# PSUM banks of one Q chunk and of the M groups assigned by hand in a fused linear-attention and MLP block

## The chip, the cores and the metric

The kernel runs on one core of one Trainium2 chip. The metric is the device time of one launch in microseconds (us).

Names used throughout: PE is TensorE (matmuls), PEld its weight loads, DVE is VectorE, ACT is ScalarE. PSUM is the memory that matmuls write; this kernel uses it as 8 banks, each of which holds a 128 x 512 fp32 result. In the lines of the chain below, "issue" is time in which an engine waited for nothing that the profile shows.

## The reference

The input is normalised, then goes through linear attention (32 heads of 20) and an MLP; both results are added to the input. Only the attention branch matters here.

```python
phi = lambda t: jnp.where(t > 0, t + 1, jnp.exp(t)) + 1e-6
pq, pk = phi(q), phi(k)
kv  = jnp.einsum("bhsd,bhse->bhde", pk, v)
z   = jnp.einsum("bhsd->bhd", pk)
num = jnp.einsum("bhqd,bhde->bhqe", pq, kv)
den = jnp.einsum("bhqd,bhd->bhq", pq, z)[..., None] + 1e-6
o   = num / den                                   # then o @ wo
# out = x + attention(xn) + mlp(xn), S = 2048, D = 640, F = 1536
```

The kernel never forms `o`: it multiplies the masked `kv` by `wo` first ("M", 640 x 640), so that `num @ wo` becomes `pq @ M` and can share an accumulation with the second MLP product.

## The kernel before

A planner records each operation with what it reads and writes, and puts a semaphore wait wherever an engine needs another's result or reuses its space. A PSUM bank is one of the tracked areas: a matmul that writes a bank waits until everything that read the bank's earlier content is done. `take(n)` hands banks out in a ring.

```python
ring = [0]
def take(n):
    b = ring[0]
    if n == 2 and b % 2:
        b += 1
    b %= 8
    ring[0] = (b + n) % 8
    return b
```

The part between the KV statistics and the output products:

```python
def phi(src, b, nb, dst, res_dst, extra_w):       # cut: index arithmetic
    Pl.ins("scalar", ... activation(e2, src, ACT.Exp), reads=br, ...)            # L463, reads the bank
    Pl.ins(v, ... tensor_scalar(et, et, 1.0, 1e-6, ALU.min, ALU.add), ...)       # L464
    Pl.ins(v, ... scalar_tensor_tensor(out=d2, in0=src, scalar=0.0, in1=e2,
           op0=ALU.max, op1=ALU.add), reads=br + [r_ek[s]], ...)                 # L466, frees the bank

def q_chunk(c):                                    # one chunk = 512 tokens, DT = 5 units
    for j in range(DT):
        b = take(1)
        Pl.ins("tensor", [5 matmuls of 128x512 into bank b], ...)                # L509
        phi(bank(b), b, 1, PQ[:, j, cc], r_PQ[c][j], [])

def z_step():                                      # cut
    ...                                            # L517, then five products ZB on DVE, L523
def kvt_step():                                    # five blocks, one bank each
    ...                                            # L529 on PE, masked copies on DVE, L533

def m_step():
    for j in range(DT):
        b = take(2)                                # a pair of banks for each of 5 groups
        ...                                        # 16 matmuls into 32-partition strips, L545
        Pl.ins("scalar", ... activation(halves(Msb[:, j, :]), pair(b), ACT.Copy),
               reads=B_[b:b + 2], writes=[r_M[j], r_zsum, r_zhl])                # L550, frees the pair

q_chunk(0); z_step(); kvt_step(); q_chunk(1)
q_chunk(2)
m_step()
q_chunk(3)
...
bs = [out_w2(0)]; db = den_step()                  # output products of the MLP; den in 32-partition strips
bs += [out_w2(1), out_w2(2, 0, JT // 2)]           # then the first products with Msb
```

Of the kernel before, what the change touches and what calls it, by code (L numbers as in the profile page):

```python
# [112 lines left out]
def bass_parallel_sum__linear_attn_block__dense_activation_gelu__prompt_kernel(  # L113
# [23 lines left out]
    with contextlib.ExitStack() as es:  # L137
# [44 lines left out]
# [10 lines that stand above are left out]
        def bank(b, lo=0, hi=512):  # L192
            return ps[:, b * 512 + lo: b * 512 + hi]

        def pair(b):
            return ps[:, b * 512:(b + 2) * 512].rearrange("p (a n) -> p a n", a=2)[:, :, 0:HW]

        def halves(ap):
            return ap.rearrange("p (a n) -> p a n", a=2)
# [255 lines left out]
        def phi(src, b, nb, dst, res_dst, extra_w):  # L455
            s = ring_e[0] % 3
            ring_e[0] += 1
            w = D if nb == 2 else CW
            et = ek[:, s, 0:w]
            e2 = halves(et) if nb == 2 else et  # L460
            d2 = halves(dst) if nb == 2 else dst
            br = B_[b:b + nb]
            Pl.ins("scalar", lambda e: e.activation(e2, src, ACT.Exp), reads=br, writes=[r_ek[s]])  # L463
            Pl.ins(v, lambda e: e.tensor_scalar(et, et, 1.0, 1e-6, ALU.min, ALU.add),  # L464
                   reads=[r_ek[s]], writes=[r_ek[s]])
            Pl.ins(v, lambda e: e.scalar_tensor_tensor(out=d2, in0=src, scalar=0.0, in1=e2,  # L466
                                                       op0=ALU.max, op1=ALU.add),
                   reads=br + [r_ek[s]], writes=[res_dst] + extra_w)

        ring_e = [0]  # L470
        for t in range(NT):
            b = take(2)
# [11 lines left out]
        for f in range(DT):  # L484
            b = take(2)
# [19 lines left out]
        def q_chunk(c):  # L505
            cc = slice(c * CW, (c + 1) * CW)
            for j in range(DT):
                b = take(1)
                Pl.ins("tensor", [(lambda e, k=k, j=j, b=b: e.matmul(  # L509
                    bank(b), Wqkv[:, k, j:D:DT], xnT[:, k, cc],  # L510
                    start=(k == 0), stop=(k == DT - 1))) for k in range(DT)],
                    reads=[r_Wq] + r_xnT[c * CH:(c + 1) * CH], writes=[B_[b]])
                phi(bank(b), b, 1, PQ[:, j, cc], r_PQ[c][j], [])
# [12 lines left out]
        def kvt_step():  # L526
            for t in range(DT):
                b = take(1)
                Pl.ins("tensor", [(lambda e, k=k, b=b, t=t: e.matmul(  # L529
                    bank(b, 0, Wd[t]), Wqkv[:, k, 2 * D + t * P:2 * D + (t + 1) * P],  # L530
                    GTb[:, k, e0[t]:e1[t]], start=(k == 0), stop=(k == DT - 1))) for k in range(DT)],
                    reads=[r_Wv] + r_GT, writes=[B_[b]])
                Pl.ins(v, lambda e, b=b, t=t: e.tensor_tensor(  # L533
                    out=KVT[:, t, e0[t]:e1[t]], in0=bank(b, 0, Wd[t]), in1=maskKV[t][:], op=ALU.mult),
                    reads=[B_[b], r_masks], writes=[r_KVT])

        def m_step():
            for j in range(DT):
                b = take(2)
                fns = []  # L540
                for h in range(2):
                    for i in range(2):
                        for q in range(4):
                            c0 = j + 32 * DT * q
                            fns.append(lambda e, t=q + i, q=q, i=i, h=h, b=b, c0=c0: e.matmul(  # L545
                                bank(b + h, 0, HW)[32 * q:32 * q + 32, :],
                                KVT[:, t, c0:c0 + 31 * DT + 1:DT], Wo[:, t, h * HW:(h + 1) * HW],
                                start=(i == 0), stop=(i == 1)))
                Pl.ins("tensor", fns, reads=[r_KVT, r_Wo], writes=B_[b:b + 2])
                Pl.ins("scalar", lambda e, b=b, j=j: e.activation(halves(Msb[:, j, :]), pair(b), ACT.Copy),  # L550
                       reads=B_[b:b + 2], writes=[r_M[j], r_zsum, r_zhl])
# [47 lines left out]
        z_step()  # L599
        kvt_step()  # L600
        q_chunk(1)
        q_chunk(2)
        m_step()
        q_chunk(3)
        for c in range(NC):
            x_again(c)
# [16 lines left out]
        def out_w2(t, lo=0, hi=JT, b=None):  # L623
            b = take(2) if b is None else b
            for i in range(lo, hi):
                Pl.ins("tensor", [mm(b, t, i, 0), mm(b, t, i, 1)], reads=mm_reads(t, i), writes=B_[b:b + 2],
                       mark=(i == JT - 1))
            return b
# [41 lines left out]
        for t in range(3, NT - 1):  # L670
            b = out_w2(t)
# [45 lines left out]
```

## Time and profile before

| | before |
|---|---|
| time, median (range), 6 runs | 210.94 us (210.4 to 211.22) |
| span of the profiled run | 209.0 us |
| PE busy | 204.9 us, 98% |
| chain of waits, by engine | PE 92%, DVE 6% |

From the page of the kernel before: the span, the engines' busy time, and the chain that ended last.

```profile
span 209.0 us, 3950 instructions
...
PE 204.9 (98%) x1599; PEld 141.0 (67%) x1599; DVE 108.8 (52%) x227; ACT 75.1 (36%) x142; POOL 20.2 (10%) x61
...
PE 92%; DVE 6%; issue 1%; DVEq 0%
```

PE is the limit. What can still be saved without removing matmuls is PE's waiting, and the chain says where to look: between the first and the last few microseconds of the kernel it leaves PE for one stretch only. These are some lines of the chain of waits in order of time (start, duration, what):

```profile
111.11 0.24 DVE ZB L523
...
114.28 0.21 DVE ek L464
...
123.54 0.70 DVE PQ L466
124.24 0.14 issue
124.38 1.29 PE ps L545 x32
125.67 5.53 PE ps L509 x25
```

From the ZB products to the fourth group of M, DVE's work is back to back and PE is released by it. DVE is late because the five ZB products and five masked copies stand in its queue ahead of the phi of Q chunk 1. Now the timeline of the same stretch (start, duration, engine, line, what, how many; in brackets the engine's idle time before it and what ended it):

```profile
109.08 0.52 PE L517 MATMUL ps<-onesb,Msb 128*128 128x1 bf16 x10
111.03 10.96 PE L509 MATMUL ps<-xnT,Wqkv 128*128 128x512 bf16 x50
116.57 0.69 DVE L466 SCALAR_TENSOR_TENSOR PQ<-ps,ek 128x512 bf16<-128x512 f32 x1
121.91 1.29 PE L545 MATMUL ps<-Wo,W 128*32 128x320 bf16 x32
122.55 0.69 DVE L466 SCALAR_TENSOR_TENSOR PQ<-ps,ek 128x512 bf16<-128x512 f32 x1
123.38 0.75 PE L545 MATMUL ps<-Wo,W 128*32 128x320 bf16 x16 [0.18 <-DVE PQ L466]
123.54 0.69 DVE L466 SCALAR_TENSOR_TENSOR PQ<-ps,ek 128x512 bf16<-128x512 f32 x1
124.38 1.29 PE L545 MATMUL ps<-Wo,W 128*32 128x320 bf16 x32 [0.24 <-DVE PQ L466]
125.60 5.12 PEld L509 LDWEIGHTS ps<-xnT,Wqkv 128*128 128x128 bf16 x25 [0.25 <-issue]
142.32 4.24 PE L617 MATMUL ps<-Msb,PQ 128*128 128x320 bf16 x30
```

How to read it: Q chunks 1 and 2 run on PE without a break (111.03 on). M's groups 0 and 1 start at 121.91. Group 2 starts at 123.38, just after the phi of Q2 unit 3 ends (122.55 + 0.69 = 123.24), and group 3 at 124.38, just after that of Q2 unit 4 (124.23). From M's start to the first weights of Q chunk 3 it is 125.60 - 121.91 = 3.69 us. The line at 109.08 (the z step) and the first product with Msb at 142.32 are two marks: 33.24 us pass from one to the other.

### The profile page before, as it was taken

The page shows a single profiled execution, that of the slowest core. Times are in us where ns is not written, and L with a number is a line of the kernel's source. Part 1 is how long each engine was busy: PE and PEld are TensorE (multiplying, and loading weights), DVE is VectorE, ACT ScalarE, POOL GpSimd, SP SyncE. Part 2 cuts the span into 40 slices and gives each one's busy share as a digit, 9 for nine tenths or more (in the row PEclk, how much of TensorE's full clock was granted, in tenths as well). Part 3 has the DMA queues.
Part 4 walks back from the last instruction along what each step waited for, and adds up shares of the span by engine and source line. Part 5 has one row for each costly group of instructions (what it writes and reads, how often), then busy time and mean ns, then how long its engine had stood idle before and what let it go on. Part 6 is the DMA issues. An engine that isn't in the chain of part 4 may idle for free.

```text
span 209.0 us, 3950 instructions
## 1 busy us (share of the span) xinstructions
PE 204.9 (98%) x1599; PEld 141.0 (67%) x1599; DVE 108.8 (52%) x227; ACT 75.1 (36%) x142; POOL 20.2 (10%) x61
## 2 busy tenths in 40 slices
PE   7999999999999999999999999999999999999995
PEld 2799987444457777777756565577777777777775
DVE  4589970000008888999178975478633522523322
ACT  2689887666676444111253576100000000000000
POOL 3245568200000000000000000000000000000000
DMA  6999668997000000000000000591120111001001
GB/s 164 348 349 112 105 129 130 376 332 260 3 0 0 0 0 3 0 3 0 0 0 5 0 0 3 193 313 57 63 59 32 58 42 55 31 31 35 31 34 61
DMA packets 22507, 17.86 MB, mean 85 GB/s; under 512 B 9176, under 2 KB 22488, under 8 KB 22488
## 3 DMA queue, kind: packets, MB, share of 16 engines
q1 hardware_dynamic: 21808, 17.11, 29.1%
q10 hardware_dynamic: 680, 0.49, 0.9%
q8 instruction: 12, 0.20, 0.4%
q14 instruction: 7, 0.06, 0.1%
HBM read 12.62 MB, written 2.62 MB: 73 GB/s over the span
## 4 chain that ended last, share of the span: by engine, by line
PE 92%; DVE 6%; issue 1%; DVEq 0%
PE ps L617 33%; PE ps L355 25%; PE ps L487 10%; PE ps L476 10%; PE ps L509 5%; DVE PQ L466 3%; PE ps L298 2%; PE ps L653 2%; DVE ek L464 1%; DVE W L533 1%; PE ps L529 1%; PE ps L545 1%; DVE ZB L523 1%; PE ps L555 1%; PE ps L385 1%
## 5 line engine op out<-in xcount | busy, mean ns | idle before, releaser
L355 PE MATMUL ps<-xnT,W 128*128 128x128 bf16 (+2 forms) x435 | 52.0, 282 | 0.0
L617 PE MATMUL ps<-W,HG 128*128 128x320 bf16 x360 | 51.4, 299 | 0.0
L355 PEld LDWEIGHTS ps<-xnT,W 128*128 128x128 bf16 x435 | 35.6, 98 | 15.6
L617 PEld LDWEIGHTS ps<-W,HG 128*128 128x128 bf16 x360 | 35.1, 98 | 14.2 <-issue 0.4
L359 ACT ACTIVATE HG<-ps,b1c 128x128 bf16<-128x128 f32 (+2 forms) x87 | 40.1, 493 | 12.4 <-PE ps L355 10.3
L464 DVE TENSOR_SCALAR ek<-ek 128x512 bf16<-128x512 bf16 (+1 forms) x36 | 11.0, 305 | 42.7 <-ACT ek L463 41.6
L636 DVE TENSOR_TENSOR out_sb<-ps,xnT 128x640 bf16<-128x640 f32 x15 | 12.4, 825 | 36.2 <-PE ps L617 36.1
L463 ACT ACTIVATE ek<-ps 128x512 bf16<-128x512 f32 (+1 forms) x36 | 23.2, 645 | 20.4 <-PE ps L509 11.2
L617 PE MATMUL ps<-Msb,PQ 128*128 128x320 bf16 x150 | 22.5, 299 | 0.0
L509 PE MATMUL ps<-xnT,Wqkv 128*128 128x512 bf16 x100 | 22.1, 379 | 0.0
L476 PE MATMUL ps<-Wqkv,xnT 128*128 128x320 bf16 x160 | 21.9, 299 | 0.0
L487 PE MATMUL ps<-xPK,xn_tm 128*128 128x320 bf16 x160 | 21.9, 299 | 0.0
L476 PEld LDWEIGHTS ps<-Wqkv,xnT 128*128 128x128 bf16 x160 | 15.7, 98 | 6.2
L487 PEld LDWEIGHTS ps<-xPK,xn_tm 128*128 128x128 bf16 x160 | 15.7, 98 | 6.1
L617 PEld LDWEIGHTS ps<-Msb,PQ 128*128 128x128 bf16 x150 | 14.6, 98 | 5.7
L509 PEld LDWEIGHTS ps<-xnT,Wqkv 128*128 128x128 bf16 x100 | 11.6, 117 | 9.6 <-issue 0.2
L466 DVE SCALAR_TENSOR_TENSOR PQ<-ps,ek 128x512 bf16<-128x512 f32 x20 | 13.8, 692 | 2.1
L311 DVE BATCH_NORM_STATS2 stats<-xPK 128x6 f32<-128x320 bf16 x32 | 13.6, 466 | 2.3 <-DMA xPK<-in_A_x_dram 2.3
L466 DVE SCALAR_TENSOR_TENSOR xPK<-ps,ek 128x640 bf16<-128x640 f32 x16 | 13.2, 824 | 1.7
L497 DVE TENSOR_TENSOR Msb<-Msb,xPK 128x640 f32<-128x640 f32 x14 | 11.6, 825 | 0.5
L491 ACT ACTIVATE W<-ps 128x640 bf16<-128x640 f32 x5 | 3.5, 704 | 18.2 <-PE ps L487 14.6
L321 POOL TENSOR_TENSOR rstd<-aggr,mhalf 128x1 f32<-128x1 f32 x16 | 9.1, 568 | 8.9 <-DVE aggr L319 8.9
(68 smaller groups left out, 93.7 us busy)
## 6 DMA issues: line engine op xcount, KB each, us to landing
xnT<-in_A_x_dram SPq DMA_DIRECT2D x4, 640.0 KB, 6.2
Wqkv<-in_A_wqkv_dram SPq DMA_DIRECT2D x3, 800.0 KB, 6.7
out_dram<-out_sb SPq DMA_DIRECT2D x15, 160.0 KB, 1.8
W<-in_B_w_dram SPq DMA_DIRECT2D x1, 1920.0 KB, 15.3
W<-in_B_w_dram SPq DMA_DIRECT2D x3, 480.0 KB, 7.0
xPK<-in_A_x_dram SPq DMA_DIRECT2D x2, 640.0 KB, 9.5
Wo<-in_A_wo_dram SPq DMA_DIRECT2D x1, 800.0 KB, 10.5
xPK<-in_A_x_dram SPq DMA_DIRECT2D x4, 160.0 KB, 4.2
```

The source lines that it names most:

```text
L311: Pl.ins(v, lambda e: e.bn_stats(stats[:, s, 6 * h:6 * h + 6], x_in[:, t, h * HW:(h + 1) * HW]), reads=[r_x[t]], writes=[r_stats[s][h]])
L355: Pl.ins("tensor", [(lambda e, k=k: e.matmul(bank(b, 0, w), W1[:, k, jb * P:(jb + 1) * P], xnT[:, k, tok], start=(k == 0), stop=(k == DT - ...
L359: Pl.ins("scalar", lambda e: e.activation(HG[:, jb, tok], bank(b, 0, w), ACT.Gelu_apprx_tanh, bias=b1c[:, jb:jb + 1]), reads=[B_[b], r_b1c ...
L463: Pl.ins("scalar", lambda e: e.activation(e2, src, ACT.Exp), reads=br, writes=[r_ek[s]])
L464: Pl.ins(v, lambda e: e.tensor_scalar(et, et, 1.0, 1e-6, ALU.min, ALU.add), reads=[r_ek[s]], writes=[r_ek[s]])
L466: Pl.ins(v, lambda e: e.scalar_tensor_tensor(out=d2, in0=src, scalar=0.0, in1=e2, op0=ALU.max, op1=ALU.add), reads=br + [r_ek[s]], writes= ...
L476: fns.append(lambda e, k=k, h=h, b=b, t=t: e.matmul(bank(b + h, 0, HW), xnT[:, k, t * P:(t + 1) * P], Wqkv[:, k, D + h * HW:D + (h + 1) * ...
L487: Pl.ins("tensor", [(lambda e, t=t, h=h, b=b, f=f: e.matmul(bank(b + h, 0, HW), xn_tm[:, t, f * P:(f + 1) * P], PK[:, t, h * HW:(h + 1) * ...
L497: Pl.ins(v, lambda e, t=t: e.tensor_tensor(out=zsum, in0=zsum, in1=PK[:, t, :], op=ALU.add), reads=[r_PK[t], r_zsum], writes=[r_zsum])
L509: Pl.ins("tensor", [(lambda e, k=k, j=j, b=b: e.matmul(bank(b), Wqkv[:, k, j:D:DT], xnT[:, k, cc], start=(k == 0), stop=(k == DT - 1))) fo ...
L617: return lambda e: e.matmul(bank(b + h, 0, HW), l, r[:, h * HW:(h + 1) * HW], start=(i == 0), stop=(i == JT + DT - 1))
L636: Pl.ins(v, lambda e: e.tensor_tensor(out=halves(out_sb[:, s, :]), in0=pair(b), in1=halves(x_res[:, t, :]), op=ALU.add), reads=B_[b:b + 2] ...
```

## The change

Its intent is to spare M those two waits: its five groups turn round in three pairs, (6,7), (0,1), (2,3), none of which is held by the last two units of Q chunk 2. For that, Q2 is made to start at bank 1, so that it ends in banks 4 and 5. No instruction is added, removed or reordered.

```diff
         def m_step():
             for j in range(DT):
-                b = take(2)
+                b = (6, 0, 2, 6, 0)[j]
                 fns = []
...
         q_chunk(1)
+        ring[0] = 1
         q_chunk(2)
         m_step()
+        ring[0] = 4
         q_chunk(3)
```

The banks that follow, counted from the ring (Q3 and all later ones are the same in both):

| | Q1, units 0 to 4 | Q2, units 0 to 4 | M, pairs from |
|---|---|---|---|
| before | 7 0 1 2 3 | 4 5 6 7 0 | 2 4 6 0 2 |
| after | 7 0 1 2 3 | 1 2 3 4 5 | 6 0 2 6 0 |

## The prediction

> **What bounds the kernel.** TensorE. The page gives PE 98% busy of a 209.0 us span, and the chain of waits is 92% PE. DVE (52%) and ACT (36%) matter only where they hold a PSUM bank that PE wants. The chain leaves PE from 110.9 to 124.4 us and runs through DVE (ZB, W and PQ lines): held up by five ZB products and five masked KVT copies, DVE starts the phi of Q chunk 1 late, at 114.20, and then works at 1.00 us a unit against PE's 1.08 (25 matmuls in 5.40 us).
>
> **What the change removes.** The ring, counted by hand: Q1 has banks 7,0,1,2,3; Q2 4,5,6,7,0; M pairs 2,4,6,0,2. So M group 2 (6,7) waits for Q2 unit 3, and group 3 (0,1) for Q2 unit 4. In the timeline M starts at 121.91, groups cost about 0.51 us, group 2 starts at 123.38 and group 3 at 124.38, each 0.14 us after the DVE end that frees it (123.24, 124.23). The gaps are 0.45 and 0.49 us: 0.94 us is all there is to win. Every instruction stays.
>
> **What it adds.** With the ring at 1, Q2 has banks 1,2,3,4,5. Its units 0 to 2 reuse the banks of Q1 units 2 to 4, only three units back. PE reaches Q2 unit 0 at about 116.43, but DVE releases Q1 unit 2 at 117.26 (timeline). With 0.14 us of latency and an exposed weight load, unit 0 starts near 117.45: a new stall of 1.0 us. Units 1 and 2 (released 118.26, 119.25) are in time. M starts about 1.03 us later, near 122.94.
>
> **M afterwards.** Pairs 6,0,2,6,0. Groups 0 to 2 find free banks (group 2's are released by about 122.6). Group 3 needs pair 6 back from ACT: the copy starts 0.80 us after its group, as before, and takes 0.76 us (three in 2.29): free at 124.50, start 124.64. Group 4 needs group 1's copy, 125.26: start 125.40, where before it was 124.89. So M shrinks by 0.5 us and starts 1.0 late: Q3 starts near 126.1 instead of 125.60. Later banks are unchanged, the den step's 1.4 us of slack after Q3's last phi hides ACT's small delay, and PE has no idle time after that, so the 0.5 us reach the end.
>
> All these waits are on the critical path. Net: -0.94 removed, +1.0 at Q2 unit 0, +0.4 waiting for ACT in M: about +0.5 us.
>
> The Trainium skill, "TensorE: Matmul & The Clock Gate", gives 215.7 ns between warm 512-column matmuls, and an idle window of about 3.4 us before the clock falls. The trace agrees with the first (0.216 us); a 1 us stall should leave the granted clock at 1.00.
>
> **Prediction:** 211.3 us, 8 in 10 between 210.5 and 212.0. Faster by over 2%: 0.01; within 2%: 0.98; slower by over 2%: 0.01.
>
> **What would show it.** PE idle 0.9 to 1.05 us before Q2's first matmul, put down to DVE's PQ line; M groups 0 to 2 back to back (1.5 us); groups 3 and 4 held by ACT's Msb copies, about 0.15 and 0.25 us; M starting near 122.9 and Q3 near 126.1; the chain going through DVE to Q2 unit 0 rather than to M.
>
> **What would make it wrong.** If DVE did Q1's phi earlier than in this trace (one execution), the stall shrinks and the change wins up to 0.5 us. If my ring count is off by one, the stall is not there. The noise of single runs (210.4 to 211.22) is as large as the effect, so the measured sign may differ.

## The result, and the profile after

| | before | after |
|---|---|---|
| time, median (range), 6 runs each | 210.94 us (210.4 to 211.22) | 211.28 us (210.8 to 211.69) |
| ratio after / before, 95% interval | | 1.0019 (1.0000 to 1.0038) |
| span of the profiled run | 209.0 us | 209.5 us |
| z step to first product with Msb | 33.24 us | 33.58 us |

A ratio here is the mean time of one kernel's fast runs over the mean of the other's of the same rounds, so it is not quite the ratio of the medians quoted beside it. Counted at 2% the two are the same; the changed kernel is most likely 0.3 to 0.4 us slower (0.34 by the medians, 0.40 by the means), and the interval just touches 1.

The page after, the same parts as above:

```profile
span 209.5 us, 3939 instructions
...
PE 203.6 (97%) x1592; PEld 140.4 (67%) x1599; DVE 109.1 (52%) x227; ACT 75.0 (36%) x142; POOL 20.2 (10%) x61
...
PE 92%; DMA 3%; DVE 3%; issue 1%; SPq 0%; DVEq 0%
```

PE has 7 matmul records fewer only because some records are missing from a trace (the weight loads, x1599, are all there). DVE's share of the chain has fallen from 6% to 3%; the 3% of DMA belong to the first loads of the kernel and not to this stretch. The chain after, from the same place on:

```profile
116.76 0.70 DVE PQ L466
117.46 0.14 issue
117.59 5.56 PE ps L509 x25
123.16 3.03 PE ps L545 x80
126.19 0.18 issue
126.37 5.34 PE ps L509 x24
```

The chain now leaves DVE at the first matmul of Q2, not in M. The timeline after:

```profile
109.26 0.52 PE L517 MATMUL ps<-onesb,Msb 128*128 128x1 bf16 x10
117.59 5.56 PE L509 MATMUL ps<-xnT,Wqkv 128*128 128x512 bf16 x25 [0.83 <-DVE PQ L466]
123.09 3.10 PE L545 MATMUL ps<-Wo,W 128*32 128x320 bf16 x80
123.89 3.89 ACT L550 ACTIVATE Msb<-ps 128x640 bf16<-128x640 f32 x5
125.44 0.43 PEld L545 LDWEIGHTS ps<-Wo,W 128*32 128x32 bf16 x16 [0.29 <-ACT Msb L550]
126.12 5.12 PEld L509 LDWEIGHTS ps<-xnT,Wqkv 128*128 128x128 bf16 x25 [0.25 <-issue]
142.84 4.24 PE L619 MATMUL ps<-Msb,PQ 128*128 128x320 bf16 x30
```

(This run is 0.18 us late already at the z step, so compare differences, not clock readings.) Q2's first matmul now waits 0.83 us for DVE to finish with Q1 unit 2, whose bank 1 it reuses: M starts 123.09 - 109.26 = 13.83 us after the z step, where before it was 121.91 - 109.08 = 12.83 us: **1.00 us later**. (The bracket's 0.83 us counts from the end of the last matmul's record. The 25 records from 117.59 last 5.56 us, though 25 matmuls follow each other in 5.40, so 0.16 us of the last record lies beyond the moment when the next matmul is due: 0.83 + 0.16 = 0.99.) M itself takes 126.12 - 123.09 = 3.03 us instead of 3.69: **0.66 us shorter**. Its two waits for DVE are gone; what it has in their place is a wait for ACT, which must copy group 1 out of pair (0,1) before group 4 may use it. From Q3's first weights on nothing differs: 16.72 us to the first product with Msb in both. Net: 1.00 - 0.66 = 0.34 us lost. The difference of the medians is the same, but that is chance: single runs scatter by more.

### The profile page after: what moved, and what is told of

Same layout as the page of the kernel before. It is cut to its first block, busy times and chain, and to the rows that moved or that the text cites. A ratio compares the mean times of both kernels' runs of the same rounds, so it can differ in the third digit from the quotient of the medians.

```text
span 209.5 us, 3939 instructions
## 1 busy us (share of the span) xinstructions
PE 203.6 (97%) x1592; PEld 140.4 (67%) x1599; DVE 109.1 (52%) x227; ACT 75.0 (36%) x142; POOL 20.2 (10%) x61
## 4 chain that ended last, share of the span: by engine, by line
PE 92%; DMA 3%; DVE 3%; issue 1%; SPq 0%; DVEq 0%
PE ps L619 33%; PE ps L355 25%; PE ps L487 10%; PE ps L476 10%; PE ps L509 8%; DMA W<-in_B_w_dram 3%; PE ps L655 2%; PE ps L545 1%; DVE PQ L466 1%; DVE W L533 1%; PE ps L529 1%; DVE ZB L523 1%; PE ps L555 1%; SPq L230 0%; PE ps L339 0%
## 5 line engine op out<-in xcount | busy, mean ns | idle before, releaser
L509 PE MATMUL ps<-xnT,Wqkv 128*128 128x512 bf16 x97 | 21.6, 379 | 1.1 <-DVE PQ L466 0.8
```

The source lines that it names most:

```text
L509: Pl.ins("tensor", [(lambda e, k=k, j=j, b=b: e.matmul(bank(b), Wqkv[:, k, j:D:DT], xnT[:, k, cc], start=(k == 0), stop=(k == DT - 1))) fo ...
```

## The experiments

The theory: the change moves PE's wait for DVE from M to the start of Q2, because Q2 units 0 to 2 reuse the banks of Q1 units 2 to 4, three units back, while DVE is still behind. Rival A: what is lost is lost in M, which now turns in three pairs and waits for ACT. Rival B: a difference of 0.3 us is noise of the start or of the chip. A further question is what DVE's lag, caused by the ZB products, has to do with it.

Each kernel of the runs e1 to e10 was timed in 5 rounds beside the kernel before on its chip (11 runs of it in each of the three series; medians 210.97, 210.78 and 211.04 us). "Stretch" is the time from the z step to the first product with Msb; it is read from the trace to 0.01 us and does not contain the start of the kernel, where most of the scatter between the profiled runs arises: leaving e9 out, which is treated under e5, they reach the z step between 109.05 and 109.59 us, while what follows the stretch takes 66.6 to 66.7 us in all. The stretch of the kernel before was traced once, but its unedited parts repeat: from the z step to M's start it is 12.83 or 12.84 us in the traces of before, e2, e3, e4 and e8. The expectations of some runs speak of the time from the z step to the first output matmul instead, which is 11.29 us less both before and after.

| run | what it is | median us | ratio to before (95%) | stretch, against 33.24 |
|---|---|---|---|---|
| after | the change | 211.28 | 1.0019 (1.0000 to 1.0038) | +0.34 |
| e5_after_again | the change, again | 212.28 | 1.0055 (1.0008 to 1.0103) | +0.35 |
| e1_nearer | Q2's first bank one unit nearer | 212.15 | 1.0057 (1.0044 to 1.0069) | +1.33 |
| e2_no_stall | Q2's first three banks free, M as after | 210.25 | 0.9963 (0.9950 to 0.9976) | -0.66 |
| e3_zb_late_before | before, ZB moved on DVE | 210.32 | 0.9974 (0.9962 to 0.9986) | -0.48 |
| e4_zb_late_after | after, ZB moved on DVE | 210.43 | 0.9976 (0.9962 to 0.9990) | -0.64 |
| e9_m_group4_bank4 | after, last M group not behind ACT | 210.98 | 0.9994 (0.9957 to 1.0030) | +0.17 |
| e10_copies_overlap | after, M's copies not chained | 211.09 | 1.0013 (0.9993 to 1.0032) | +0.16 |
| e8_all_banks | all of this together | 210.08 | 0.9953 (0.9921 to 0.9985) | -0.83 |
| e7_m_beside_den | before, M moved beside den | 209.72 | 0.9938 (0.9905 to 0.9972) | -1.07 |

All gave correct results. The ratios of the series of e5, e7, e8 and e9 contain late-starting runs (see e5; the one that was profiled is late long before the edits). Without these, chosen after the fact, the ratios of e9, e8 and e7 are 1.0006, 0.9965 and 0.9951, or +0.13, -0.73 and -1.04 us.

### e1_nearer: more of the suspected stall

```diff
-        ring[0] = 1
-        q_chunk(2)
+        q_chunk(2, (2, 3, 1, 4, 5))     # q_chunk takes its banks from a list
```

> After, but Q chunk 2 in banks 2,3,1,4,5: unit 0 reuses the bank of Q1 unit 3 instead of unit 2, one unit nearer. Theory (the loss is PE waiting for the bank that DVE still holds for Q1): the stall before Q2's first matmul grows by DVE's 1.0 us a unit, from 0.8 to about 1.8 us (PE idle, released by DVE's PQ line), M takes the same 3.0 us, and the time is about 1.0 us over the changed kernel's: 212.2, ratio to before about 1.006. Rival A (M held by ACT's copies is the loss): M's pairs and copies are those of the changed kernel, so 211.3, ratio 1.002. Rival B (the difference between the two kernels is noise of the start or of the chip): 210.9 to 211.3.

PE's timeline:

```profile
118.49 5.56 PE L509 MATMUL ps<-xnT,Wqkv 128*128 128x512 bf16 x25 [1.82 <-DVE PQ L466]
123.98 3.10 PE L545 MATMUL ps<-Wo,W 128*32 128x320 bf16 x80
```

One unit nearer costs 1.82 - 0.83 = 0.99 us more of waiting, one DVE unit, and the stretch is 1.33 - 0.34 = 0.99 us longer; M is as after. The time follows: 212.15 us. Rivals A and B do not give this.

### e2_no_stall: the stall alone taken away

```diff
-        ring[0] = 1
-        q_chunk(2)
+        q_chunk(2, (6, 7, 0, 4, 5))
```

> After, but Q chunk 2 in banks 6,7,0,4,5: M keeps the changed kernel's pairs 6,0,2,6,0 and Q2's last two units keep banks 4 and 5; only units 0 to 2 move, to banks that were free for over 1 us (6, 7) or at the very moment (0). Theory: no stall before Q2, M 3.0 us from its start to Q3 (0.3 us of it waiting for ACT's copy of group 1), Q3 about 0.65 us earlier than in the kernel before, so about 210.3, ratio to before 0.997. Rival A (ACT's copies in M are the loss): M unchanged, so as slow as the changed kernel, ratio 1.002. Rival B (noise): 1.000 to 1.002.

PE's timeline:

```profile
109.34 0.52 PE L517 MATMUL ps<-onesb,Msb 128*128 128x1 bf16 x10
111.50 10.74 PE L509 MATMUL ps<-xnT,Wqkv 128*128 128x512 bf16 x49
122.17 3.10 PE L545 MATMUL ps<-Wo,W 128*32 128x320 bf16 x80
```

Q1 and Q2 are one unbroken piece again (x49, one record missing), M starts 12.83 us after the z step as before the change, and M has exactly the changed kernel's pairs and length (3.03 us from its start to Q3's first weights). The time is 210.25 us, 0.7 us under before, interval clear of 1. So M's new pairs are a gain of 0.66 us, and the three banks of Q2's first units turned it into a loss. Rival A falls as the explanation of the loss.

### e3_zb_late_before and e4_zb_late_after: DVE's lag taken away, with both assignments

```diff
         q_chunk(2)
+        zb_step()                # the five products of L523, taken out of z_step
         m_step()
```

> The kernel before with its own banks, the five ZB products moved on DVE from before Q1's phi to behind Q2's (where DVE idles 3.3 us). Theory: DVE is no longer 1.3 us behind, so PE's wait at M group 2 vanishes, at group 3 about 0.4 us stay (Q2 unit 4's phi), Q3 begins about 0.5 us earlier: about 210.4, ratio 0.9975. If DVE's lag has no part in it: ratio 1.000.

> The changed kernel with the same move of the ZB products. Theory: DVE releases Q1 unit 2 about 116.2 instead of 117.3, before PE wants its bank, so the stall at Q2 unit 0 vanishes and only M's 0.3 us of waiting for ACT stays: about 0.65 us under before, 210.25, ratio 0.997; so the bank change that costs about 0.35 us with the ZB products early gains about 0.15 us with them late. Rival A (ACT's copies in M are the loss): the changed banks still lose 0.3 us against e3, ratio about 0.999.

PE's timeline, first of e4, then of e3:

```profile
111.75 10.75 PE L509 MATMUL ps<-xnT,Wqkv 128*128 128x512 bf16 x49
...
121.98 3.26 PE L547 MATMUL ps<-Wo,W 128*32 128x320 bf16 x80
125.18 5.12 PEld L509 LDWEIGHTS ps<-xnT,Wqkv 128*128 128x128 bf16 x25 [0.25 <-ACT Msb L552]
```

With the ZB products out of its way DVE frees Q1 unit 2 at 116.79 in e4, 0.15 us before Q2's first matmul (116.94): just in time, with nothing to spare. PE's Q1 and Q2 are one piece, and M is 3.03 us long. In e3, M takes 125.18 - 121.98 = 3.20 us: one wait, for Q2 unit 4, is left of the two. Both times fall as expected, to 210.32 us (e3) and 210.43 us (e4). The finer claim, that the same bank change which loses 0.34 us with ZB early gains with ZB late, shows in the stretch (-0.64 against -0.48 us, 0.16 us), but not in the times, whose order is the reverse and whose intervals overlap widely: the profiled run of e4 reached its z step 0.44 us later than that of e3, before any edited instruction. The times cannot settle 0.16 us.

### e5_after_again: is it noise?

The changed kernel, unedited.

> The changed kernel once more, unedited, for a second interval. Theory: 0.34 us over before (22.29 against 21.95 us from the z step to the first output matmul), ratio 1.0016. Rival B (noise): the sign changes, ratio at or below 1.000.

The stretch is 33.59 us, the stall 0.82 us: the same as in the first trace. The ratio of 1.0055 is too large to be the change: three of the six runs took 213.1 to 213.3 us, the other three 211.05 to 211.42; one of the 11 runs of the kernel before in the same series took 213.18. Leaving those four out, chosen after the fact, the means are 211.24 and 210.81, a difference of 0.42 us before rounding. Rival B falls for the stretch, on two traces, but the time alone would not have refuted it.

Where the 2.4 us of such a run come from can be seen in the profile of e9, which fell into one (213.4 us). Windows of one microsecond, with PE busy first and the granted clock (PEclk) third from the right:

```profile
core 0: us, PE busy (x) PEld busy (x) DVE busy (x) ACT busy (x) POOL busy (x), PEclk, DMA share, GB/s
7.00:8.00 1.00, 0.03 (x1) 0.03 (x2) 0.04 (x1) 0.42 (x2) 0.00 (x0) 1.00 1.09 373
8.00:9.00 1.00, 1.00 (x14) 1.00 (x15) 0.00 (x0) 0.28 (x1) 0.00 (x0) 0.74 1.10 337
9.00:10.00 1.00, 1.00 (x12) 1.00 (x11) 0.11 (x1) 0.73 (x3) 0.00 (x0) 0.50 1.09 338
10.00:11.00 1.00, 1.00 (x12) 1.00 (x11) 1.00 (x3) 0.41 (x2) 0.13 (x1) 0.50 1.09 331
11.00:12.00 1.00, 1.00 (x13) 1.00 (x11) 0.90 (x4) 0.69 (x2) 0.52 (x2) 0.55 1.08 353
12.00:13.00 1.00, 1.00 (x21) 1.00 (x19) 0.81 (x3) 0.97 (x4) 0.44 (x3) 1.00 1.07 364
```

PE waits 1.04 us for the first W1 load (to 7.97), and from about 8.5 us on the clock runs at half for about 3.4 us (the missing clock is 0.26 + 0.50 + 0.50 + 0.45 = 1.71 us of full speed). It is over before 13 us, and the z step comes at 111.63 instead of about 109.2. That is 100 us ahead of the change and has nothing to do with it. That the other late runs are of this kind is likely, as they are late by much the same amount (1.9 to 2.4 us) and their recorded mean clock is 0.992, as in e9, but they were not profiled. That the wait brought the clock down is not shown either: it came just before.

### e9_m_group4_bank4 and e10_copies_overlap: the wait for ACT in M

e9 puts M's last group in the pair that Q2's last units leave; e10 leaves the pairs and lets the copies follow one another faster.

```diff
e9:
-                b = (6, 0, 2, 6, 0)[j]
+                b = (6, 0, 2, 6, 4)[j]
...
-        ring[0] = 4
+        ring[0] = 0
         q_chunk(3)
e10:
-                       reads=B_[b:b + 2], writes=[r_M[j], r_zsum, r_zhl])
+                       reads=B_[b:b + 2], writes=[r_M[j]] + ([r_zsum, r_zhl] if j == 0 else []))
```

> After, with M's last group in the pair (4,5) instead of (0,1), so that it waits for the phi of Q2 unit 4 (done about 0.1 us before it is wanted) and not for ACT's copy of group 1; Q chunk 3 then starts at bank 0 so that it does not meet that pair. Theory: the 0.3 us of ACT in M go, the 0.8 us stall at Q2 stays: 22.0 us from the z step to the first output matmul instead of 22.29, time equal to before, ratio 1.000. This measures the ACT term alone; were it the whole loss and more (rival A), the ratio would fall to about 0.997.

> After, with M's copies 1 to 4 no longer declared as writers of the old zsum and zhl space that Msb takes over (copy 0 alone still is, and waits for their last readers). In the trace of after, the five copies start 0.80 us apart, (3.89 - 0.70)/4, though one takes 0.704: each waits for the one before it on ScalarE itself, because all five write the same two tracked areas. Theory: without that wait they follow at 0.70 us or less, group 1's pair comes back at least 0.19 us earlier, and M takes about 2.87 us instead of 3.03; the stall at Q2 stays; 0.17 us over before: ratio 1.000 to 1.001, the time itself hardly resolvable, the trace decides. If the spacing is ScalarE's own and no wait, it stays at 0.80 and M at 3.03.

PE's timeline of e10:

```profile
123.19 2.92 PE L545 MATMUL ps<-Wo,W 128*32 128x320 bf16 x80
126.04 5.12 PEld L509 LDWEIGHTS ps<-xnT,Wqkv 128*128 128x128 bf16 x25 [0.25 <-issue]
```

Both bring M to 2.85 us from its start to Q3's first weights (in e10 126.04 - 123.19, in e9 128.31 - 125.46), with no wait for ACT left, and both leave the 0.83 us at Q2. So the ACT term is 3.03 - 2.85 = 0.18 us; 0.29 us, the idle time of the weight loads before group 4, was too high a reading of it. ACT in e10:

```profile
123.99 3.09 ACT L550 ACTIVATE Msb<-ps 128x640 bf16<-128x640 f32 x5
```

Against 3.89 us for the five after. A copy takes 0.70 us; the starts are (3.09 - 0.70) / 4 = 0.60 us apart instead of 0.80. All five copies had been recorded as writers of the same two old areas, so each waited on ACT's own semaphore for the one before, although they write different columns. Both effects on the time are below what the intervals resolve; the traces decide here.

### e8_all_banks: all terms together, order of PE unchanged

```diff
-                b = (6, 0, 2, 6, 0)[j]
+                b = (6, 0, 2, 6, 4)[j]
...
-        ring[0] = 1
-        q_chunk(2)
+        q_chunk(2, (6, 7, 0, 4, 5))
+        zb_step()
         m_step()
-        ring[0] = 4
+        ring[0] = 0
```

> After with all three terms taken away: Q2 in banks 6,7,0,4,5 (no stall at its start), M's pairs 6,0,2,6,4 (last group not behind ACT), ZB products behind Q2 (so that the phi of Q2 unit 4 is done in time for that), Q3 from bank 0. Theory: M about 2.75 us from its start to Q3, no other wait: 21.0 us from the z step to the first output matmul, 0.95 us under before: 210.0, ratio 0.9955.

M takes 125.08 - 122.23 = 2.85 us, there is no other wait, and the stretch is 0.83 us shorter than before. 0.95 was expected, because M without waits had been put at 2.75 us instead of 2.85. The table's ratio meets the expected 0.9955 only with the late run of the kernel before; without it the time is 0.73 us under before.

### e7_m_beside_den: the waits designed away

```diff
         q_chunk(2)
-        m_step()
         q_chunk(3)
...
-        bs = [out_w2(0)]
-        db = den_step()
-        bs += [out_w2(1), out_w2(2, 0, JT // 2)]
+        m_step((0, 1, 2, 3))            # pairs 6, 0, 2, 6
+        ring[0] = 4
+        db = den_step()
+        m_step((4,))                    # pair 0
+        bs = [out_w2(0, b=2), out_w2(1, b=6), out_w2(2, 0, JT // 2, b=0)]
+        ring[0] = 4
```

> The kernel before with M moved behind Q chunk 3, next to the den step that also writes 32-partition strips: groups 0 to 3 (pairs 6,0,2,6), den in bank 4, group 4 (pair 0), then the output products. No Q unit's bank is held when M wants it, den's 1 us lets ACT catch up before group 4, and one change between strip and full-width matmuls goes. Theory: all 0.94 us of M's gaps and about 0.25 us of a change go: 1.2 us under before, 209.75, ratio 0.9943.

PE's timeline:

```profile
109.05 0.53 PE L517 MATMUL ps<-onesb,Msb 128*128 128x1 bf16 x10
...
111.22 16.14 PE L509 MATMUL ps<-xnT,Wqkv 128*128 128x512 bf16 x73
127.28 2.38 PE L545 MATMUL ps<-Wo,W 128*32 128x320 bf16 x64
129.49 1.25 PE L555 MATMUL ps<-PQ,ZB 128*32 128x512 bf16 x20
130.56 0.72 PE L545 MATMUL ps<-Wo,W 128*32 128x320 bf16 x16
131.21 10.17 PE L616 MATMUL ps<-W,HG 128*128 128x320 bf16 x72
141.22 4.24 PE L616 MATMUL ps<-Msb,PQ 128*128 128x320 bf16 x30
```

Three Q chunks, M, den and the output products follow without a recorded wait. The stretch is 1.07 us shorter and the time 209.72 us, the best of all: each of its six runs (209.31 to 210.16) is under the fastest of the kernel before in that series (210.58). Of the 1.07 us, 0.84 is what M's waits cost before (3.69 - 2.85); that the other 0.23 come from one change fewer between strip and full-width matmuls was expected, but was not separated by a run.

## Why the prediction was right

- **What bounds it.** Right: PE, with DVE mattering only as the holder of banks. e3 and e4, which move nothing but five small DVE products, save 0.48 us of the stretch and, on the changed banks, 0.34 + 0.64 = 0.98 us.
- **Removed: 0.94 us of waits in M.** Right in place, somewhat high: 3.69 - 2.85 = 0.84 us. M without waits had been put at 2.75 us, with its groups 0.51 us apart; in e10, where none waits, the first matmuls of groups 0 and 4 start at 123.19 and 125.39, which is 0.55 us from group to group.
- **Added: a stall of about 1.0 us at Q2 unit 0.** Right: M starts 1.00 us later (1.03 predicted). The recorded idle time of 0.83 us lies outside the 0.9 to 1.05 named as a sign, because it counts from the end of the last record (see above). The released bank was Q1 unit 2's, e1 shows the DVE unit of 0.99 us as its step, and e2 removes it.
- **Added: 0.4 us of waiting for ACT in M.** Right in kind, over twice too high: 0.18 us (e9, e10). This is the term that was mis-sized most. Group 3 was to wait 0.15 us for its pair and did not: it starts 0.54 us after group 2 (124.75 against 124.21), as without waits, for the copy of group 0 had ended at 124.59. Group 4 did wait, but it starts at 125.44, 0.05 us after the copy of group 1 (124.69 + 0.70 = 125.39), where the prediction had added the 0.14 us seen after DVE. That group would have been due 0.54 us after group 3, at 125.29, so it waited about 0.15 us.
- **Sum.** -0.84 + 1.00 + 0.18 = +0.34 us in place of the predicted +0.5; 211.28 us measured against 211.3. Q3's first weights come 16.86 us after the z step, where 17.0 was predicted. The errors of the two terms in M, +0.10 and -0.22 us, partly cancelled. That the median came so near is luck: the noise of the times is as large as the effect, as the prediction said.
- **Clock.** As predicted, the stall did not lower it: the clock in the windows around it, 111 to 123 us, is 1.00; it is 1.00 too from 111 to 125 us of e1, whose stall is 1.82 us. The Trainium skill, "TensorE: Matmul & The Clock Gate", "Back-to-back issue gap", gives N / 2.4 + 2.5 ns as the gap of a warm matmul taken by itself (215.8 ns for 512 columns, an estimate by this formula), and about 131 ns for a sustained stream with weight loads; the trace, which is such a stream, agrees with the first and not with the second: 25 in 5.40 us, 216 ns each.

## What to carry to other kernels

In a ring of PSUM banks it is not enough that all banks are in use: what counts is how long ago the bank's last reader was due when PE comes back to it, and a reader that lags shortens that for every user. The Trainium skill, "Perfetto Trace Analysis", "Matmul Optimizations", advises using all 8 banks; the kernel before and the changed one both do, and so does e2, yet the stretch differs by 1.0 us between the last two. Before reassigning banks to spare one wait, list for each user the time at which its bank is released against the time at which PE arrives, for the donors as well as for the receiver; then ask whether the lagging reader can be relieved, or the step moved to where nobody holds its banks, which here gave more than any assignment (what its lead of 0.24 us over e8 comes from is not shown).

## What the Trainium skill lacked or had wrong

- "TensorE: Matmul & The Clock Gate", "What's actually happening": the table has the clock fall after at least one idle window of about 3.4 us. It does not say how busy PE may be in a window that still counts as idle. In the profile of e9 the clock fell to 0.50 for about 3.4 us although PE had waited only 1.04 us at a stretch and had been busy for 1.75 us of 3.40 (4.8 to 8.2). The busy time alone does not decide it: around the stall of e1 PE was busy for only 1.58 us of 3.40 (115.1 to 118.5), and the clock stayed at 1.00. What decides stays open.
- "ScalarE: Activation LUTs", "What ACT_TABLE_LOAD costs": an ACTIVATE with immediate operands is given as 186 ns + 0.833 ns per element, which makes 719 ns for 640 (an estimate by this formula), and back-to-back ones as overlapping by about 93 ns. The trace agrees within 5%: 704 ns, and starts 0.60 us apart in e10, where 719 - 93 makes 0.63. The page lacks what a wait on the engine's own semaphore does to that: 0.80 us apart, the overlap gone and about 0.1 us added.
- No page gives the delay from the end of a reader's record to the matmul that waits for it. It was not one figure here: 0.14 us from the end of DVE's record to PE's next matmul (before: 123.24 to 123.38; the chain after: 117.46 to 117.59), but 0.05 us from the end of ACT's copy to M's group 4 (after: 125.39 to 125.44).
